# Linear attention with decay, then two MLP layers, one core: the second batch's heads of a pair exchanged

## The chip, the cores and the metric

One core of a Trainium2 chip. The metric is the device time of one execution in microseconds: median of three runs of the kernel before 559.44 us (559.34 to 560.02).

## The reference

Causal linear attention with a decay per head (2 batches, 8 heads, 768 positions, 64 channels), then two MLPs with 1536 tokens, width 512 and inner width 2048. In the reference the attention goes in blocks of 64 positions:

```python
intra = np.einsum('bhic,bhjc->bhij', qb, kb) * Dmask[None]
intra = np.einsum('bhij,bhjd->bhid', intra, vb)
inter = np.einsum('bhid,bhde->bhie', qb * lam_pow[None], kv_state)
out[:, :, sl] = intra + inter
kb_dec = kb * rev_pow[None]
kv_state = lam_block[None, :, None, None] * kv_state + np.einsum('bhsd,bhse->bhde', kb_dec, vb)
...
x = attn_out.transpose(0, 2, 1, 3).reshape(B * S, H * D)
h = x @ w_in
g = np.where(h > 0.0, h, alpha * (np.exp(np.minimum(h, 0.0)) - 1.0))
x = g @ w_out
```

`Dmask` is the head's decay `lam` to the power of the distance, zero ahead of the diagonal; the second MLP has a leaky rectifier with a slope per column in place of the exponential.

## The kernel before

**Attention.** Each batch is cut into six blocks of 128 positions; the two blocks of the same position, one of each batch, are a unit (`units`, m = 0 to 5). The host lays out keys and queries with the channels on the partitions: a pair of heads fills 128 partitions, 64 each, and `kqT` has for every block four pairs of keys and of queries (512 KB); `vk` has values and keys with the positions on the partitions (512 KB). For a unit TensorE makes:
- `scores` (L616, products L625): keys times queries, 64 channels deep, so two heads work in the two row halves of the array, each into its own bank of PSUM; VectorE multiplies with the decay masks `dm` into `sm` (L631).
- `state` (L656, L667): scaled keys `kd` times values, 64 by 64 for each head, added up in bank `SUMS`; two heads in the two column halves.
- `new_states` (L673): ScalarE or VectorE copies the sums into `st`, ScalarE multiplies the sums in PSUM by the block's decay (`decay`, L688).
- `outputs` (L691, L700): `sm` times values, two heads in the two column halves, one group for each batch, into banks `OUTS`.
- `earlier` (L707, L720): the state times the queries scaled by the decay (`qs`, L651 on GpSimd), added onto the same banks. Here `st` holds for each pair a 128 by 128 matrix with the two heads' 64 by 64 blocks on its diagonal and zeros beside them (cleared once, L762), so one product over the whole array serves both heads. Then ScalarE casts the bank to the high part of x (L419) and VectorE subtracts it for the low part (L737).

All of these are float32 products, each seen in the trace as two records. The MLP products (L872, L904, L969) use rounded high and low parts of x and weights.

**Start.** `begin` (L748) loads `lam`, spreads it with small products (L771, L773) behind six warm-up products (L609), makes the masks on VectorE (L785), gets their last row by a product (L795) and from it the query scales `qp` (L791).

**Order.** Every piece is an `Op` with a cost per engine. The planner (`Plan`) computes by when each is needed and simulates the engines; TensorE takes from the ready pieces the one needed first, and a change between kinds of array division (`mode`: full, rows, cols) costs it `CHANGE` more but is not avoided. Loads stand on the SP queue in turn: for each unit two of `kqT`, two of `vk`; only the second block's first load is on ScalarE's queue. Behind the loads of unit 3 come the first two weight loads of 1 MB (`raw`), then units 4 and 5. The first MLP's products for the chunks of units 0 to 3 are mixed into the attention; those of the third chunk (units 4 and 5, `x0`) follow it. The MLPs then run to the end.

## Time and profile before

| | |
|---|---|
| median of 3 runs | 559.44 us (559.34 to 560.02) |
| profiled execution: its time, its span | 559.58 us, 557.8 us |
| TensorE busy | 550.8 us (99%) |
| VectorE, ScalarE, GpSimd busy | 385.7, 297.8, 319.9 us |
| granted clock of TensorE | 1.00 throughout |
| chain that ended last | PE 89%, DMA 5%, VectorE 3%, ACT 2% |

An engine's busy time is the time in which at least one of its instructions runs; for TensorE ends are modelled, so the distance from start to start of two groups is what a group costs. Float32 products have two records each: 16 products are x32. The chain shows which engine the end waited for, going back step by step.

### The profile page before, as it was taken

The page shows a single profiled execution, that of the slowest core. Times are in us where ns is not written, and L with a number is a line of the kernel's source. Part 1 is how long each engine was busy: PE and PEld are TensorE (multiplying, and loading weights), DVE is VectorE, ACT ScalarE, POOL GpSimd, SP SyncE. Part 2 cuts the span into 40 slices and gives each one's busy share as a digit, 9 for nine tenths or more (in the row PEclk, how much of TensorE's full clock was granted, in tenths as well). Part 3 has the DMA queues.
Part 4 walks back from the last instruction along what each step waited for, and adds up shares of the span by engine and source line. Part 5 has one row for each costly group of instructions (what it writes and reads, how often), then busy time and mean ns, then how long its engine had stood idle before and what let it go on. Part 6 is the DMA issues. An engine that isn't in the chain of part 4 may idle for free.

```text
span 557.8 us, 7420 instructions
## 1 busy us (share of the span) xinstructions
PE 550.8 (99%) x2872; PEld 456.9 (82%) x2872; DVE 385.7 (69%) x499; ACT 297.8 (53%) x488; POOL 319.9 (57%) x222
## 2 busy tenths in 40 slices
PE   8999999999999999999999999999999999999997
PEld 6888888888888888888888887888888888888886
DVE  5688999487576867577856794649676757774554
ACT  4686776666465746556646537644454435434220
POOL 4544532676657574929368588577666583927020
PEclk9999999999999999999999999999999999999999
DMA  8992222220404132221310120032222222000114
GB/s 330 404 363 76 76 75 76 76 77 0 152 0 152 49 103 75 76 76 55 128 45 13 63 76 1 23 130 76 75 77 75 76 75 76 0 1 0 39 38 150
DMA packets 18309, 49.24 MB, mean 88 GB/s; under 512 B 1250, under 2 KB 1506, under 8 KB 18274
## 3 DMA queue, kind: packets, MB, share of 16 engines
q1 hardware_dynamic: 18128, 48.25, 24.4%
q8 instruction: 22, 0.36, 0.3%
q10 hardware_dynamic: 146, 0.52, 0.3%
q14 instruction: 13, 0.11, 0.1%
HBM read 45.62 MB, written 3.15 MB: 87 GB/s over the span
## 4 chain that ended last, share of the span: by engine, by line
PE 89%; DMA 5%; DVE 3%; ACT 2%; issue 1%; ACTq 0%; SPq 0%
PE ps L969 46%; PE ps L904 23%; PE ps L872 18%; DMA blk<-in_kqT 3%; DMA raw<-in_w1o 2%; PE ps L720 1%; PE ps L700 1%; DVE qT2l L427 1%; PE ps L625 1%; DVE g L427 1%; DVE wt L461 0%; DVE acc L981 0%; PE ps L667 0%; DVE rt L834 0%; ACT rt L817 0%
## 5 line engine op out<-in xcount | busy, mean ns | idle before, releaser
L981 DVE TENSOR_TENSOR acc<-ps,acc 128x512 f32<-128x512 f32 (+1 forms) x169 | 115.8, 687 | 93.7 <-PE ps L969 92.6
L427 POOL TENSOR_TENSOR g<-rt,g 128x512 fp32r<-128x512 f32 x86 | 123.0, 1436 | 73.6 <-ACT g L419 65.2
L969 PE MATMUL ps<-wdh,g 128*128 128x512 f32 (+1 forms) x388 | 118.5, 387 | 0.0
L969 PE MATMUL ps<-g,wdh 128*128 128x512 f32 x384 | 118.2, 389 | 0.0
L817 ACT ACTIVATE rt<-ps 128x512 f32<-128x512 f32 x96 | 57.2, 597 | 96.5 <-DVE ps L918 54.7
L969 PEld LDWEIGHTS ps<-wdh,g 128*128 128x128 f32 x388 | 72.7, 188 | 14.9
L969 PEld LDWEIGHTS ps<-g,wdh 128*128 128x128 f32 x384 | 72.1, 188 | 15.0
L419 ACT CAST g<-rt 128x512 fp32r<-128x512 f32 x96 | 59.4, 619 | 40.9 <-DVE rt L834 28.3
L969 PE MATMUL ps<-wdl,g 128*128 128x512 f32 (+1 forms) x194 | 75.0, 387 | 0.0
L969 PE MATMUL ps<-g,wdl 128*128 128x512 f32 x192 | 74.7, 389 | 0.0
L427 POOL TENSOR_TENSOR wsl<-wt,wsh 128x1024 fp32r<-128x1024 f32 x13 | 32.3, 2486 | 46.3 <-ACT wsh L419 28.5
L834 DVE SCALAR_TENSOR_TENSOR rt<-rt,beta,ps 128x512 f32<-128x512 f32 x48 | 35.6, 742 | 24.7 <-ACT rt L817 24.7
L427 POOL TENSOR_TENSOR wdl<-wt,wdh 128x1024 fp32r<-128x1024 f32 x14 | 38.4, 2746 | 20.7 <-ACT wdh L419 20.5
L461 DVE SCALAR_TENSOR_TENSOR wt<-raw,wt 128x1024 uint32<-128x1024 uint32 x32 | 45.5, 1426 | 0.0
L918 DVE TENSOR_TENSOR ps<-ps,ut 128x512 f32<-128x512 f32 x42 | 29.3, 698 | 22.8 <-PE ps L904 18.6
L427 POOL TENSOR_TENSOR wt<-wt 128x256 f32<-128x256 f32 x52 | 40.1, 784 | 8.4 <-DVE wdl L427 5.6
L458 DVE SCALAR_TENSOR_TENSOR wt<-raw,wt 128x1024 uint32<-128x1024 uint32 x32 | 42.8, 1338 | 0.2
L969 PEld LDWEIGHTS ps<-wdl,g 128*128 128x128 f32 x194 | 36.4, 188 | 7.3
L969 PEld LDWEIGHTS ps<-g,wdl 128*128 128x128 f32 x192 | 36.0, 188 | 7.5
L419 ACT COPY ut<-ps 128x512 f32<-128x512 f32 x42 | 24.6, 587 | 31.3 <-PE ps L904 31.0
L453 ACT ACTIVATE wt<-raw 128x1024 f32<-128x1024 f32 x32 | 36.6, 1143 | 8.9 <-POOL wt L427 4.1
L872 PE MATMUL ps<-x0l,wah 128*128 128x512 f32 x128 | 38.6, 389 | 0.0
(128 smaller groups left out, 929.2 us busy)
## 6 DMA issues: line engine op xcount, KB each, us to landing
raw<-in_w1i SPq DMA_DIRECT2D x8, 1024.0 KB, 5.7
raw<-in_w1o SPq DMA_DIRECT2D x8, 1024.0 KB, 4.9
raw<-in_w2i SPq DMA_DIRECT2D x8, 1024.0 KB, 5.4
raw<-in_w2o SPq DMA_DIRECT2D x8, 1024.0 KB, 4.8
blk<-in_kqT SPq DMA_DIRECT2D x11, 512.0 KB, 11.4
blk<-in_vk SPq DMA_DIRECT2D x10, 512.0 KB, 11.6
out<-acc SPq DMA_DIRECT2D x11, 256.0 KB, 2.0
blk<-in_kqT ACTq DMA_DIRECT2D x1, 512.0 KB, 4.8
```

The lines of the kernel that those rows point to most:

```text
L419: nc.scalar.copy(dst(), src())
L427: lambda e: on(e).tensor_tensor(out=dst(), in0=a(), in1=b(), op=alu),
L453: op({"ACT": 1.14}, lambda e: nc.scalar.mul(t, upper.bitcast(F32), 2.0 ** -112), [b_r], [b_t])
L458: op({"DVE": vec(1024)}, lambda e: nc.vector.scalar_tensor_tensor(out=tu, in0=lower, scalar=29, in1=tu, op0=ALU.logical_shift_right, op1=A ...
L461: op({"DVE": vec(1024)}, lambda e: nc.vector.scalar_tensor_tensor(out=tu, in0=upper, scalar=0x80000000, in1=tu, op0=ALU.bitwise_and, op1=A ...
L817: op({"ACT": act(512, True)}, lambda e: nc.scalar.activation(rt(i), h(), AF.Relu, scale=-1.0), [b_h], [b_r])
L834: op({"DVE": vec(512) + 0.06}, lambda e: nc.vector.scalar_tensor_tensor(out=rt(i), in0=rt(i), scalar=beta[:, f:f + 1], in1=h(), op0=ALU.mu ...
L872: nc.tensor.matmul(out=banks[k], lhsT=wa(s, w)[:, cc, q * 128:(q + 1) * 128], rhs=(both[t][x] if t else x0(x))[:, cc, :], start=i == 0, st ...
L904: nc.tensor.matmul(out=banks[k], lhsT=left(s, a, w)[:, cc, :], rhs=quad(b, x)[:, cc, :], start=bool(opens and i == 0), stop=bool(closes an ...
L918: op({"DVE": vec(512)}, lambda e: nc.vector.tensor_tensor(out=banks[to], in0=banks[k], in1=ut(u), op=ALU.add), [b_ps[k], b_ut[u]], [b_ps[to]])
L969: nc.tensor.matmul(out=p_, lhsT=lhs, rhs=rhs, start=i == 0, stop=i == 5)
L981: op({"DVE": vec(w)}, lambda _, a=a, p_=p_: nc.vector.tensor_tensor(out=a(), in0=p_, in1=a(), op=ALU.add), [b_ps[k], *b_a], b_a)
```

## The change

The heads of a pair are exchanged for the second batch: head `hs` lies on partitions `half(hs ^ b)`. A head's state is kept as its 64 by 64 block alone; the product with the queries uses a quarter of the array for each head and batch, so that the two batches and two heads of a pair fill four quarters (`earlier`; five groups of 16 products for ten of 4). Scores are cut into halves of the keys in the same way (12 groups of 16 products for 12 of 8). The states are copied in one instruction; the decay takes eight instructions of 64 columns for four of 128; masks' last row and query scales are made once for each batch. The second batch's keys and queries come in two loads of 64 partitions, all on the SP queue, with `alpha` behind unit 3; half of the warm-up products follow the spreading of `lam`. The planner lets TensorE prefer a piece of the present mode if it is needed at most `STAY` (2 us) later than another.

```diff
-    FREE = True
+    STAY = 2.0
...
-                if e == "PE" and self.FREE:
-                    while ready[e]:
-                        op = heapq.heappop(ready[e])[2]
-                        if op not in begun:
...
                 if e == "PE":
-                    if at < len(pe) and not left[pe[at]]:
-                        shift = now - first[pe[at]]
-                        begin(e, pe[at])
-                        at += 1
+                    queue = [item for item in ready[e] if item[2] not in begun]
+                    if queue:
+                        op = min(queue, key=lambda item: (
+                            item[0] + self.STAY * (item[2].mode != mode), item[1]))[2]
+                        shift = now - first[op]
+                        ready[e] = [item for item in queue if item[2] is not op]
+                        begin(e, op)
...
-    lams_sb = sb("lams_sb", [H + NP])
-    lam_sb, lamp = lams_sb[:, 0:H], lams_sb[:, H:H + NP]
+    lams_sb = sb("lams_sb", [H + B * NP])
+    lam_sb, lamp = lams_sb[:, 0:H], lams_sb[:, H:].rearrange("p (b a) -> p b a", b=B)
...
-    st = low[:, 2:4].rearrange("p b (a i) -> p b a i", a=NP)
+    st = low[:, 2].rearrange("p (b a d) -> p b a d", b=B, a=NP)
     top = sb("qpsm", [3, 512], F32, "ut")
-    qp = top[:, 0].rearrange("p (a i) -> p a i", a=NP)
-    lamc = qp[:, :, C - 1:C]
+    qps = [x.rearrange("p (a i) -> p a i", a=NP) for x in (top[:, 0], low[:, 3])]
...
-
-        def load_kq(self, queue="SP"):
-            load(self.kq, kqT[self.n], 0.5, [self.b_kq], queue, True)
-
-        def load_vk(self, queue="SP"):
+            self.rows = [half(hs ^ b) for hs in range(2)]
+
+        def load_kq(self):
+            if self.n < PB:
+                load(self.kq, kqT[self.n], 0.5, [self.b_kq], turn_=True)
+                return
+            parts = []
+            for hs in range(2):
+                x = Buf()
+                x.wrote, x.read = list(self.b_kq.wrote), list(self.b_kq.read)
+                load(self.kq[self.rows[hs]], kqT[self.n, half(hs)], 0.25, [x], turn_=True)
+                parts += x.wrote
+            self.b_kq.wrote, self.b_kq.read = parts, []
+
+        def load_vk(self):
             n = 1 if self.n % PB == PB - 1 else 2
-            load(self.vk[:, 0:n], vk[self.n, :, 0:n], 0.25 * n, [self.b_v], queue, True)
...
-                    for hs in range(2):
+                    for hs, s in ((0, 0), (1, 1), (0, 1), (1, 0)):
                         nc.tensor.matmul(
-                            out=banks[ks[hs]][:, pr * C:(pr + 1) * C],
-                            lhsT=x.kq[half(hs), 0, pr, :], rhs=x.kq[half(hs), 1, pr, :],
-                            start=True, stop=True)
-            pe(0.89, run, [x.b_kq], [b_ps[k] for k in ks], 32, "rows")
+                            out=banks[ks[hs]][half(s), pr * C:(pr + 1) * C],
+                            lhsT=x.kq[x.rows[hs], 0, pr, half(s)],
+                            rhs=x.kq[x.rows[hs], 1, pr, :], start=True, stop=True)
+            pe(0.86, run, [x.b_kq], [b_ps[k] for k in ks], 64, "quarters")
...
-                        in0=x.kq[:, 1], in1=qp, op=ALU.mult)
-                op(SCALE, queries, [x.b_kq, b_qp], [b_qs[m % 2][b]], True)
+                        in0=x.kq[:, 1], in1=qps[b], op=ALU.mult)
+                op(SCALE, queries, [x.b_kq, b_qp[b]], [b_qs[m % 2][b]], True)
...
-                            out=view[half(hs), b, pr, :],
+                            out=view[x.rows[hs], b, pr, :],
...
-        parts = []
-        for hs in range(2):
-            x = Buf()
-            x.wrote, x.read = list(b_st.wrote), list(b_st.read)
-            copy(lambda hs=hs: st[half(hs), :, :, half(hs)], lambda hs=hs: view[half(hs)],
-                 [b_ps[SUMS]], [x], 512, True)
-            parts += x.wrote
-        b_st.wrote, b_st.read = parts, []
+        copy(lambda: st, lambda: view, [b_ps[SUMS]], [b_st], 512, True)
         if m < UNITS - 2:
             def decay(e):
-                for pr in range(NP):
-                    nc.scalar.mul(view[:, :, pr, :], view[:, :, pr, :], lamc[:, pr, :])
-            op({"ACT": 1.05}, decay, [b_ps[SUMS], b_qp], [b_ps[SUMS]])
+                for b in range(B):
+                    for pr in range(NP):
+                        nc.scalar.mul(view[:, b, pr, :], view[:, b, pr, :], qps[b][:, pr, C - 1:C])
+            op({"ACT": 1.6}, decay, [b_ps[SUMS], *b_qp], [b_ps[SUMS]])
...
-        for b in range(B):
-            k = ks[b]
-            if m:
-                def run(b=b, k=k):
-                    for pr in range(NP):
-                        nc.tensor.matmul(
-                            out=banks[k][:, pr * C:(pr + 1) * C], lhsT=st[:, b, pr, :],
-                            rhs=qss[m % 2][:, b, pr * C:(pr + 1) * C],
-                            start=False, stop=True, skip_group_check=True)
-                pe(0.88, run, [b_st, b_qs[m % 2][b]], [b_ps[k]], 16)
+        if m:
+            def run():
+                for pr in range(NP):
+                    for hs in range(2):
+                        for b, x in enumerate(units[m]):
+                            nc.tensor.matmul(
+                                out=banks[ks[b]][half(hs), pr * C:(pr + 1) * C],
+                                lhsT=st[x.rows[hs], b, pr, :],
+                                rhs=qss[m % 2][x.rows[hs], b, pr * C:(pr + 1) * C],
+                                start=False, stop=True, skip_group_check=True)
+            pe(0.86, run, [b_st, *b_qs[m % 2]], [b_ps[k] for k in ks], 64, "quarters")
+        for b, k in enumerate(ks):
...
-        op({"POOL": 1.1}, lambda e: nc.gpsimd.memset(st, 0.0), [], [b_st])
...
-            for hs in range(2):
-                nc.tensor.matmul(
-                    out=p_[half(hs), H:H + NP], lhsT=row[:, 0:64],
-                    rhs=lams.rearrange("p (a s) -> p s a", s=2)[:, hs], start=True, stop=True,
-                    skip_group_check=True)
-        pe(0.4, spread, [b_row, b_one], [b_ps[k]])
-        run_up(3)
-        op({"DVE": 0.17}, lambda e: nc.vector.tensor_copy(lams_sb, p_[:, 0:H + NP]),
+            for b in range(B):
+                for hs in range(2):
+                    nc.tensor.matmul(
+                        out=p_[half(hs ^ b), H + b * NP:H + (b + 1) * NP], lhsT=row[:, 0:64],
+                        rhs=lams.rearrange("p (a s) -> p s a", s=2)[:, hs], start=True, stop=True,
+                        skip_group_check=True)
+        plan.behind(pe(0.4, spread, [b_row, b_one], [b_ps[k]]), run_up(3))
+        op({"DVE": 0.17}, lambda e: nc.vector.tensor_copy(lams_sb, p_[:, 0:H + B * NP]),
...
-        def powers(e):
-            for pr in range(NP):
-                nc.scalar.mul(qp[:, pr], p2[:, pr * C:(pr + 1) * C], lamp[:, pr:pr + 1])
-
-        def last_row():
-            for hs in range(2):
-                nc.tensor.matmul(
-                    out=p2[half(hs)], lhsT=last_key, rhs=dm[:, hs].rearrange("p a i -> p (a i)"),
-                    start=True, stop=True, skip_group_check=True)
         for hs in range(2):
             op({"DVE": 1.3}, lambda e, hs=hs: masks(e, hs), [b_lam, b_anti], [b_dm[hs]], True)
-        k2 = turn("ps", 8)
-        p2 = banks[k2]
-        pe(1.0, last_row, [*b_dm, b_last], [b_ps[k2]], 8, "cols")
-        op({"ACT": 1.05}, powers, [b_ps[k2], b_lam], [b_qp])
-        load(alpha_sb, alpha, 0.01, [b_alpha])
+        for b in range(B):
+            k = turn("ps", 8)
+            p2 = banks[k]
+
+            def last_row(b=b, p2=p2):
+                for hs in range(2):
+                    nc.tensor.matmul(
+                        out=p2[half(hs ^ b)], lhsT=last_key,
+                        rhs=dm[:, hs].rearrange("p a i -> p (a i)"), start=True, stop=True,
+                        skip_group_check=True)
+
+            def powers(e, b=b, p2=p2):
+                for pr in range(NP):
+                    nc.scalar.mul(qps[b][:, pr], p2[:, pr * C:(pr + 1) * C], lamp[:, b, pr:pr + 1])
+            pe(0.9, last_row, [*b_dm, b_last], [b_ps[k]], 8, "cols")
+            op({"ACT": 1.05}, powers, [b_ps[k], b_lam], [b_qp[b]])
...
         def fetch(m):
-            for i, x in enumerate(units[m]):
-                x.load_kq("ACT" if m == 0 and i else "SP")
+            for x in units[m]:
+                x.load_kq()
             for x in units[m]:
                 x.load_vk()
         begin()
         for m in range(4):
             fetch(m)
+        load(alpha_sb, alpha, 0.01, [b_alpha], turn_=True)
```

TensorE's queue, the piece with the state products of units 1 and 2 (scores L625, outputs L700, states L667, state products L720); before:

```order
L720 MATMUL ps<-qs,dmst 128x128 x4
L667 MATMUL ps<-blk,kd 64x64 x16
L625 MATMUL ps<-blk 128x128 x8
L720 MATMUL ps<-qs,dmst 128x128 x4
L625 MATMUL ps<-blk 128x128 x8
L700 MATMUL ps<-sm,blk 64x128 x8
L625 MATMUL ps<-blk 128x128 x8
L700 MATMUL ps<-sm,blk 64x128 x8
L720 MATMUL ps<-qs,dmst 128x128 x4
L667 MATMUL ps<-blk,kd 64x64 x16
L720 MATMUL ps<-qs,dmst 128x128 x4
L700 MATMUL ps<-qpsm,blk 64x128 x8
```

and now (scores L630, outputs L699, states L672, state products L719):

```order
L630 MATMUL ps<-blk 64x128 x32
L699 MATMUL ps<-sm,blk 64x128 x8
L672 MATMUL ps<-blk,kd 64x64 x16
L719 MATMUL ps<-qs,dmst 64x128 x16
L630 MATMUL ps<-blk 64x128 x32
L699 MATMUL ps<-sm,blk 64x128 x16
L719 MATMUL ps<-qs,dmst 64x128 x16
L672 MATMUL ps<-blk,kd 64x64 x16
L699 MATMUL ps<-qpsm,blk 64x128 x8
L699 MATMUL ps<-sm,blk 64x128 x8
L719 MATMUL ps<-qs,dmst 64x128 x16
L672 MATMUL ps<-blk,kd 64x64 x16
```

The state products of both batches stand in one group, and groups of scores and of outputs stand together.

ScalarE's queue around the casts of units 1 and 2 (key scaling L641, casts L419, decay L688); before:

```order
L641 ACTIVATE kd<-blk,dmst 128x64 x8
L419 CAST qbh<-ps 128x4x128
L419 COPY dmst<-ps 64x8x64
L419 CAST qbh<-ps 128x4x128
L641 ACTIVATE kd<-blk,dmst 128x64 x8
L688 ACTIVATE ps<-ps,qpsm 128x2x64 x4
L453 ACTIVATE wt<-raw 128x1024
L419 CAST qbh<-ps 128x4x128
```

and now (key scaling L646, casts L411, decay L687):

```order
L646 ACTIVATE kd<-blk,dmst 128x64 x8
L411 CAST qbh<-ps 128x4x128 x2
L687 ACTIVATE ps<-ps,qpsm 128x64 x4
L687 ACTIVATE ps<-ps,dmst 128x64 x4
L646 ACTIVATE kd<-blk,dmst 128x64 x8
L411 CAST qbh<-ps 128x4x128 x2
L445 ACTIVATE wt<-raw 128x1024
L687 ACTIVATE ps<-ps,qpsm 128x64 x4
```

Both casts of a unit stand together, and those of unit 2 stand behind eight key scalings (of unit 3).

SP's queue from its start; before:

```order
L407 DMA alpha_sb<-in_alpha 128x16
L407 DMA blk<-in_kqT 128x1024
L407 DMA blk<-in_vk 128x1024 x2
L407 DMA blk<-in_kqT 128x1024 x2
L407 DMA blk<-in_vk 128x1024 x2
L407 DMA blk<-in_kqT 128x1024 x2
```

and now:

```order
L399 DMA blk<-in_kqT 128x1024
L399 DMA blk<-in_kqT 64x1024 x2
L399 DMA blk<-in_vk 128x1024 x2
L399 DMA blk<-in_kqT 128x1024
L399 DMA blk<-in_kqT 64x1024 x2
L399 DMA blk<-in_vk 128x1024 x2
```

Keys of both batches come first, the second's in two loads of 64 partitions, and `alpha` has gone behind unit 3.

## Rows read from the trace of the kernel before

**Rows 1.** Windows of core 0: length, busy us by engine (records), granted clock, DMA share, GB/s.

```profile
0.00:5.80 5.80, 3.66 (x18) 3.32 (x18) 1.11 (x5) 1.49 (x2) 1.87 (x9) 1.00 0.63 213
5.80:58.18 52.38, 51.16 (x664) 43.47 (x665) 40.94 (x62) 35.18 (x90) 27.19 (x20) 1.00 0.77 300
58.18:100.00 41.82, 41.82 (x185) 34.46 (x184) 39.52 (x48) 30.43 (x51) 14.54 (x10) 1.00 0.19 64
```

**Rows 2.** Timeline, TensorE: start us, us, line, shape, records, wait; the start.

```profile
1.18 2.93 PE L609 MATMUL ps<-warm 128*128 128x128 f32 x12 [1.18 <-DVE warm L750]
4.04 0.59 PE L771 MATMUL ps<-row 1*128 1x8 f32 x2
...
5.80 2.06 PE L625 MATMUL ps<-blk 64*128 64x128 f32 x32 [0.96 <-DMA blk<-in_kqT]
7.79 1.14 PE L795 MATMUL ps<-dmst,last_key 128*64 128x512 f32 x4
```

**Rows 3.** Timeline, TensorE, the end of the attention stage.

```profile
50.70 1.15 PE L667 MATMUL ps<-blk,kd 128*64 128x64 f32 x32
51.69 1.05 PE L700 MATMUL ps<-qpsm,blk 128*64 128x128 f32 x16
52.56 1.04 PE L700 MATMUL ps<-sm,blk 128*64 128x128 f32 x16
...
55.34 1.17 PE L872 MATMUL ps<-qbh,wah 128*128 128x512 f32 x4
...
58.18 1.07 PE L872 MATMUL ps<-x0h,wah 128*128 128x512 f32 x4
```

**Rows 4.** Waits to 60 us, TensorE's: who for whom, us in total, times, longest.

```profile
PE ps L625 <- DMA blk<-in_kqT: 1.4, 3, 1.0
...
PE ps L667 <- ACT ps L688: 0.3, 1, 0.3
...
PE ps L700 <- DVE sm L631: 0.2, 1, 0.2
```

**Rows 5.** Windows of core 0, columns as in rows 1, two while all loads run.

```profile
20.00:25.00 5.00, 5.00 (x86) 4.57 (x88) 2.88 (x5) 3.25 (x12) 3.60 (x3) 1.00 1.03 399
25.00:30.00 5.00, 5.00 (x82) 4.35 (x79) 3.43 (x7) 4.14 (x12) 1.06 (x1) 1.00 1.04 407
```

**Rows 6.** Timeline, TensorE: state products (L720) and unit 4's first scores.

```profile
18.79 1.16 PE L720 MATMUL ps<-qs,dmst 128*128 128x128 f32 x8
19.88 1.15 PE L667 MATMUL ps<-blk,kd 128*64 128x64 f32 x32
...
32.03 1.16 PE L625 MATMUL ps<-blk 64*128 64x128 f32 x16 [0.23 <-DMA blk<-in_kqT]
...
45.97 2.05 PE L720 MATMUL ps<-qs,dmst 128*128 128x128 f32 x16
47.78 1.17 PE L872 MATMUL ps<-qbh,wah 128*128 128x512 f32 x4
```

**Rows 7.** Timeline, VectorE: the masks, and a subtraction of low parts.

```profile
5.16 2.63 DVE L785 TENSOR_TENSOR_SCAN dmst<-lams_sb,anti 128x128 f32<-128x128 f32 x8
...
25.31 0.68 DVE L737 TENSOR_TENSOR qbl<-ps,qbh 128x512 fp32r<-128x512 f32 x1
```

**Rows 8.** Timeline, GpSimd: key scaling of unit 3.

```profile
25.58 1.06 POOL L644 TENSOR_TENSOR kd<-blk,dmst 128x512 f32<-128x512 f32 x1 [0.96 <-DMA blk<-in_vk]
```

**Rows 9.** Timeline, ScalarE: powers, cast of an output, key scaling, decay.

```profile
9.42 1.11 ACT L791 ACTIVATE qpsm<-ps,lams_sb 128x128 f32<-128x128 f32 x4
...
23.78 0.58 ACT L419 CAST qbh<-ps 128x512 fp32r<-128x512 f32 x1
24.26 2.02 ACT L641 ACTIVATE kd<-blk,dmst 128x64 f32<-128x64 f32 x8
26.18 1.44 ACT L688 ACTIVATE ps<-ps,qpsm 128x128 f32<-128x128 f32 x4
```

**Rows 10.** The page, DMA issues: KB each, median us from issue to landing.

```profile
blk<-in_kqT SPq DMA_DIRECT2D x11, 512.0 KB, 11.4
```

More of the change, by code (lines that the diff above doesn't have):

```diff
@@ L120, in simulate @@
     def simulate(self, first, back=False, log=None):
-        pe = self.pe[::-1] if back else self.pe
         before = (lambda op: op.after) if back else (lambda op: op.before)
@@ L131, in simulate @@
         events, begun, n = [], {}, 0
-        at, done, now, dma, shift = 0, 0, 0.0, 0.0, -first[pe[0]]
+        done, now, dma, shift = 0, 0.0, 0.0, -first[self.pe[-1 if back else 0]]
         stock, seen, mode = self.AHEAD, 0.0, None
@@ L137, in offer @@
             for e in op.costs:
-                if e != "PE" or self.FREE:
-                    heapq.heappush(ready[e], (first[op], n, op))
-                    n += 1
+                heapq.heappush(ready[e], (first[op], n, op))
+                n += 1
         def wake(t, what=None):
@@ L184, in simulate @@
                     continue
-                if e == "PE" and self.FREE:
-                    while ready[e]:
-                        op = heapq.heappop(ready[e])[2]
-                        if op not in begun:
-                            shift = now - first[op]
-                            begin(e, op)
-                            break
-                    continue
-                if e == "PE":
-                    if at < len(pe) and not left[pe[at]]:
-                        shift = now - first[pe[at]]
-                        begin(e, pe[at])
-                        at += 1
+                if e == "PE":
+                    queue = [item for item in ready[e] if item[2] not in begun]
[5 more added lines that the diff above has]
+                        begin(e, op)
                     continue
@@ L573, in attention_two_layers @@
     b_dm = [Buf(), Buf()]
-    b_qp, b_lam, b_anti, b_warm, b_row = (Buf() for _ in range(5))
+    b_qp = [Buf() for _ in range(B)]
+    b_lam, b_anti, b_warm, b_row = (Buf() for _ in range(4))
     SUMS = 6
@@ L584, in attention_two_layers, with half @@
     PART = [1, 1, 2, 2, 0, 0]
+    def half(x):
+        return slice(x * 64, (x + 1) * 64)
     class Block:
@@ L593, in __init__ @@
             self.n = PB * b + m
-        def load_kq(self, queue="SP"):
-            load(self.kq, kqT[self.n], 0.5, [self.b_kq], queue, True)
-        def load_vk(self, queue="SP"):
+            self.rows = [half(hs ^ b) for hs in range(2)]
[11 more added lines that the diff above has]
+        def load_vk(self):
             n = 1 if self.n % PB == PB - 1 else 2
-            load(self.vk[:, 0:n], vk[self.n, :, 0:n], 0.25 * n, [self.b_v], queue, True)
+            load(self.vk[:, 0:n], vk[self.n, :, 0:n], 0.25 * n, [self.b_v], turn_=True)
     units = [[Block(m, b) for b in range(B)] for m in range(UNITS)]
@@ L610, in run @@
                     out=banks[k][:, 0:128], lhsT=warm, rhs=warm, start=True, stop=True)
-        pe(0.22 * n, run, [b_warm, *reads], [b_ps[k]])
-    def half(x):
-        return slice(x * 64, (x + 1) * 64)
+        return pe(0.22 * n, run, [b_warm, *reads], [b_ps[k]])
     def scores(m):
@@ L1076, in build @@
             for e in range(4):
-                b_acc[0, e, q].read += old(*b_dm, b_st)
+                b_acc[0, e, q].read += old(*b_dm, b_st, b_qp[1])
         for b in b_ut:
-            b.read += old(b_qp, *b_sm[2])
+            b.read += old(b_qp[0], *b_sm[2])
         b_wa[1][1].read += old(*b_sm[3])
```

## The prediction

> **What bounds the kernel now.** I read the windows first [rows 1]. From 58.18 us on TensorE works without a gap (41.82 us busy of 41.82 to 100 us), so whatever is taken from TensorE's work ahead of 58.18 us moves the end by the same amount, unless something new makes it wait. Ahead of that lies the attention stage, from the first scores at 5.80 us [rows 2] to the first product of the third token chunk at 58.18 us [rows 3]: 52.38 us, in which TensorE is busy for 51.16. The reader is to see that this stage is also bound by TensorE, but only just. The waits there [rows 4] are small (1.4 us for `kqT`, 0.96 of it ahead of the first scores, 0.3 for ACT's decay, 0.2 for the masked scores), yet the DMA engines are full (share 1.03, 399 GB/s from 20 to 25 us [rows 5]), and the scores of unit 4 begin the moment their keys land, at 32.03 us [rows 6]. So less work on TensorE is a gain as far as the loads let it through.
>
> **Prices.** State products (L720): two groups of four take 47.78 − 45.97 = 1.81 us, 0.905 a group [rows 6]. Alone, between other kinds of product, a group takes 19.88 − 18.79 = 1.09 us [rows 6]; the 0.185 us more is the price of a change of the array's division. The other ends of that price: a group at L667 costs 50.70 to 51.69 = 0.99 where the next has the same division, and 1.09 − 0.99 is about 0.1. I take 0.185, the price at the very groups that change, and keep 0.1. Outputs (L700): 52.56 − 51.69 = 0.87; states (L667): 0.99 for 32 records [rows 3]. Scores (L625): two groups in 7.79 − 5.80 = 1.99 with one change, so 0.90 each [rows 2].
>
> A group in quarters is in no row. Sixteen products of 128 columns, four at a time, stream for as long as eight that go two at a time: 0.87 to 0.90. It issues 32 records, and L667's 32 records need 0.99, so that is the other end for full concurrency. I take 0.93, nearer to the streams since these have 128 columns and not 64. If only two quarters run at a time, it is 1.8, twice a group of scores (a rival below).
>
> **The sum, part by part.**
> 1. State products: ten groups at 0.905 become five at 0.93: 9.05 − 4.65 = −4.4 us.
> 2. Scores: twelve groups from 0.90 to 0.93: +0.4 (ends −0.4 and +1.1).
> 3. The second product of the masks' last row (L795): 1.14 us for both heads with its end [rows 2], 0.95 without it: +0.95.
> 4. Changes of division between the first scores and the third W1 tile of the stage: I count 33 in the order before and 23 in the new one (11 and 7 in the pieces shown with the change). Ten at 0.185: −1.85 (end −1.0).
> 5. Start. The first 5.80 us move 213 GB/s [rows 1], 1.24 MB, of which the first two loads of keys are 1.05. Now these stand first in one queue, with no `alpha` ahead of them and no values beside them: 0.19 MB at 399 GB/s is 0.5 us. Half of the 2.93 us of warm-up goes behind the lam product (4.04 us [rows 2]), so the masks (5.16 to 7.79 us [rows 7]) start up to 1.4 us earlier too. I take −0.5; ends 0 and −1.0.
> 6. Waits. Before, the work in the stage is 10.8 scores + 0.95 + 10.44 outputs (12 × 0.87) + 4.95 states + 9.05 + the three W1 tiles (36 products; one takes 58.18 − 55.34 = 2.84 us [rows 3], 0.1 of it the change ahead: 8.2 in all) + 33 × 0.185 = 50.5 us; the stage lasts 52.38, so 1.9 are waits, listed or too short to be. After, the same list gives 11.16 + 1.9 + 10.44 + 4.95 + 4.65 + 8.2 + 4.26 = 45.6. New waits come from the loads: 2.1 MB a unit at 399 GB/s is 5.3 us, while a unit now needs some 6.2 us of TensorE (two scores 1.86, two outputs 1.74, state 0.99, state products 0.93, 3.5 changes 0.65), so only the first units and unit 4 meet them. And one comes from ACT's queue: its casts of unit 2 stand behind eight key scalings of unit 3, as today, but are wanted sooner. The scalings wait for values landing at 25.58 us (POOL's L644 of the same unit ends its wait there [rows 8]). 25.58 + 2.02 (L641) + two casts of 0.58 [rows 9] + VectorE's L737, 0.68 [rows 7], is 29.4 us, less the 0.5 of the start: 28.9. Only then is the output bank free for unit 3. TensorE gets there at 5.3 + 8 × 0.93 + 1.9 + 6 × 0.87 + 3 × 0.99 + 2 × 0.93 + 11 × 0.185 = 26.7 us, with a microsecond of waits for the keys of units 1 and 2 at 27.7: a wait of 1.2 more. I put the new waits at 3.0 in place of 1.9: +1.1 (ends 0 and +2.5).
>
> Sum: −4.4 + 0.4 + 0.95 − 1.85 − 0.5 + 1.1 = **−4.3 us**.
>
> What costs nothing: ACT's decay becomes eight instructions of half the width; four take 1.44 us [rows 9], so eight lie between 1.44 and 2.9, one more microsecond on the way from one state to the next, of which one copy of 0.58 is given back. TensorE waits for the decay 0.3 us in all today [rows 4], so this hides; without that cover it would be 0.4 to 0.9 us a unit. The second powers (L791, 1.11 us [rows 9]) stand ahead of ACT's first cast, where the keys of unit 1 are waited for anyway. SP issues seven loads more (six by the halving, one that was ACT's), and its loads of keys are issued 11.4 us ahead of their landing [rows 10]. GpSimd's clearing of the states stood ahead of an idle stretch.
>
> The profiled execution took 559.58 us (span 557.8), 0.14 above the median of 559.44. 559.58 − 4.3 is 555.3, or **555.2** against the median. Its own range, from the ends above: 553.4 to 557.3.
>
> **Rivals.**
> *The half loads run at half rate.* Each 512 KB of the second batch's keys is now two loads onto 64 rows. A 128-row load takes 1.31 us at 399 GB/s. If a half, which reaches half of the rows, is no faster than that, each unit gets 1.31 us longer, 6.6 us until both halves for unit 4 are there: 32.03 + 1.3 (the second batch) − 0.5 + 6.6 = 39.4 us. After that there remain three groups of scores, four of outputs, a state, two groups of state products, eight changes and the three W1 tiles: 2.8 + 3.5 + 1.0 + 1.9 + 1.5 + 8.2 = 18.9. That ends at 58.3, where TensorE stands today at 58.18: the whole gain is gone, **560** with a wait or two. For it: nothing in the trace, which has no 64-row load. Against it: the rate is the same 399 to 407 GB/s whether keys, values or weights are moved, in loads of 512 KB or 1 MB [rows 5], so bytes alone have set it so far. Since no row decides it and any rate between is possible, I give it 0.27, over 557.5 to 561. The Trainium skill has a rule that is this rival ("SBUF — State Buffer", Door 1: The DMA port swizzle): 64 rows reach half of the ports, and two transfers onto the two halves serialize. By that rule the time is the 560; no run here shows it yet.
>
> *Quarters run only two at a time* (the rival that ends slower). Place: every group of scores, 12 × (1.8 − 0.9) = +10.8; state products 5 × 1.8 against 9.05, no gain; +0.95 − 1.85 − 0.5, and about 1 us of waits less: +8.4, **568**. It decides from about 1.2 us a group on. For it: no row has rows and columns divided at once. Against it: L625 divides rows, L700 columns, and both run two at a time. In part it may hold for the state products alone, whose two row halves write one bank in turn: then only the 4.4 us go, 559. The Trainium skill has a rule of that kind ("TensorEngine Tiling (Array Packing)", Gotcha 1: PSUM Pressure: different row tiles cannot access the same bank at the same time); by it the time is that 559, and nothing in the trace speaks to it. 0.06 for each.
>
> *VectorE becomes the bound.* From 58.18 to 100 us it is busy 39.52 of 41.82 us [rows 1], so TensorE, 4 us ahead, may run into it: in full that takes back 2 to 4 us, **557.5 to 559.5**. Against it: VectorE is idle for a fifth of the stage before (40.94 of 52.38 [rows 1]) and no wait for it is seen today. 0.10.
>
> *The change doesn't do what it says:* that the new order brings none of the merging is excluded by its rows; 0.01.
>
> **How the numbers follow.** Forecast 0.50. A measurement of this kernel tells 0.2% (1.1 us) from no change, so faster is below 558.3. Forecast 0.50, a third of the half-rate case (0.09), two thirds of VectorE's (0.07): 0.66. Same: 0.10 of the half-rate case, the rest of VectorE's and the one-bank case: 0.19. Slower: 0.08 of the half-rate case and the quarters, 0.15. The range 553.4 to 560.6 leaves out the quarters, the end of the half-rate case and a few hundredths below.
>
> **What would show it.** Right: first scores near 5.3 us; a group of 32 state-product records and of 32 score records at 0.93, 1.1 with a change; outputs of unit 3 waiting for L738 about a microsecond; the stage over near 54 us; no gap behind it. Wrong: waits of TensorE for `kqT` of a microsecond or more in each unit (half rate), quarter groups of 1.3 us or more, or gaps behind 60 us that VectorE ends.

## The result and the profile after

The changed kernel takes **568.36 us** (median of 5 runs, 566.43 to 569.45) against 559.65 for the kernel before beside it: a ratio of 1.0150 (95% interval 1.0132 to 1.0169), 8.7 us slower. The forecast was 555.2 us with a range up to 560.6: the time went the other way and left the range. The profiled execution took 569.45 us.

The page of the changed kernel: span, busy times, the rate in 40 slices of the span, the chain that ended last, and the loads of keys and queries (KB each, median us to landing):

```profile
span 566.5 us, 8025 instructions
...
PE 551.4 (97%) x3152; PEld 455.2 (80%) x3152; DVE 393.7 (69%) x501; ACT 301.1 (53%) x509; POOL 320.8 (57%) x220
...
GB/s 264 292 319 242 48 67 75 75 75 74 2 148 93 56 75 74 75 75 76 76 146 1 75 67 8 2 148 5 144 75 74 75 74 75 1 1 0 38 38 148
...
PE 82%; DMA 9%; DVE 5%; issue 1%; ACT 1%; SPq 1%; ACTq 0%; DVEq 0%
...
blk<-in_kqT SPq DMA_DIRECT2D x6, 512.0 KB, 10.1
blk<-in_kqT SPq DMA_DIRECT2D x12, 256.0 KB, 12.5
```

TensorE is busy about as long as before (550.8 then), the span is 8.7 us longer: the time went into waiting. The chain's share of DMA rose from 5 to 9%. A load of half the bytes lands later after its issue (12.5 us) than one of 512 KB before (11.4 [rows 10]).

TensorE's waits in it to 82 us (who waited for whom: us in total, times, longest; those under 0.6 left out):

```profile
PE ps L630 <- DMA blk<-in_kqT: 3.7, 5, 1.7
PE ps L672 <- issue: 1.9, 1, 1.9
PE ps L699 <- DVE qbl L738: 1.5, 1, 1.5
...
PE ps L630 <- DVE qpsm L636: 0.9, 1, 0.9
PE ps L874 <- DVE rt L832: 0.8, 2, 0.5
PE ps L874 <- DVE x0l L738: 0.7, 1, 0.7
PE ps L971 <- DVE rt L832: 0.6, 1, 0.6
```

Where [rows 4] had 1.4 us for `kqT` there are 3.7, and a new kind: "issue", a gap for which the profile shows no releaser.

Its timeline of TensorE (start us, us, line, operands, records, wait ahead):

```profile
5.38 3.76 PE L630 MATMUL ps<-blk 64*64 64x128 f32 x64
9.07 2.04 PE L797 MATMUL ps<-dmst,last_key 128*64 128x512 f32 x8
...
15.46 1.15 PE L672 MATMUL ps<-blk,kd 128*64 128x64 f32 x31
18.49 0.27 PE L672 MATMUL ps<-blk,kd 128*64 128x64 f32 x1 [1.88 <-issue]
...
19.66 3.79 PE L630 MATMUL ps<-blk 64*64 64x128 f32 x64
23.39 1.09 PE L699 MATMUL ps<-sm,blk 128*64 128x128 f32 x16
...
33.50 1.10 PE L719 MATMUL ps<-qs,dmst 64*64 64x128 f32 x32
34.53 1.15 PE L672 MATMUL ps<-blk,kd 128*64 128x64 f32 x32
...
49.08 1.10 PE L630 MATMUL ps<-blk 64*64 64x128 f32 x32 [1.66 <-DMA blk<-in_kqT]
...
64.90 1.07 PE L874 MATMUL ps<-x0h,wah 128*128 128x512 f32 x4
66.64 1.20 PE L874 MATMUL ps<-x0l,wah 128*128 128x512 f32 x4 [0.67 <-DVE x0l L738]
```

A state-product group of 32 records takes 34.53 − 33.50 = 1.03 us with its change of division, 0.85 without (0.185): four quarters do run at once, since two at a time would be some 1.8. The third chunk's first product starts at 64.90 us, 6.7 later than in [rows 3]. The gap of 1.88 us stands in the middle of one group, 31 records ahead of it and one behind, and the profile shows nothing that this one record waited for. And the scores at 19.66 us take 3.73 for what takes 1.9 elsewhere: the granted clock there is the next view's.

Windows of the changed kernel (columns as in [rows 1]): just behind that gap; a 128-row load of keys; the two 64-row loads behind it; two weight loads. Which load runs follows from the bytes moved in the order of issue.

```profile
19.00:22.00 3.00, 3.00 (x52) 2.69 (x51) 0.30 (x1) 2.69 (x9) 1.45 (x2) 0.59 1.01 318
...
22.20:23.40 1.20, 1.20 (x32) 1.03 (x24) 0.79 (x2) 0.67 (x3) 0.89 (x1) 0.68 1.06 416
23.60:26.00 2.40, 2.26 (x56) 2.05 (x56) 1.18 (x2) 1.15 (x5) 1.06 (x1) 1.00 1.03 191
30.00:35.00 5.00, 4.80 (x110) 4.07 (x112) 1.39 (x3) 2.86 (x11) 2.29 (x2) 1.00 1.05 398
```

The DMA engines are full in all four (1.01 to 1.06). The 64-row loads move 191 GB/s, the 128-row load and the weights 416 and 398: each engine is as busy and moves half. (The first window, with 318, has the end of two half loads and values in it.) By the DMA view about as many packets pass in the 2.40 us of the 64-row loads (139) as in the 1.20 us of the 128-row one (133). After 1.88 us without work the granted clock fell (0.59 from 19 to 22 us: mostly 1.2 GHz, the lower of the two levels).

### The profile page after: what moved, and what is told of

Read it like the earlier page. It is cut to its first block, busy times and chain, and to the rows that moved or that the text cites. A ratio compares the mean times of both kernels' runs of the same rounds, so it can differ in the third digit from the quotient of the medians.

```text
span 566.5 us, 8025 instructions
## 1 busy us (share of the span) xinstructions
PE 551.4 (97%) x3152; PEld 455.2 (80%) x3152; DVE 393.7 (69%) x501; ACT 301.1 (53%) x509; POOL 320.8 (57%) x220
## 4 chain that ended last, share of the span: by engine, by line
PE 82%; DMA 9%; DVE 5%; issue 1%; ACT 1%; SPq 1%; ACTq 0%; DVEq 0%
PE ps L971 45%; PE ps L906 23%; PE ps L874 14%; DMA blk<-in_kqT 5%; DMA raw<-in_w1i 2%; DMA blk<-in_vk 2%; DVE g L419 1%; DVE wt L453 1%; SPq L399 1%; DVE qT2l L419 1%; DVE x0l L738 0%; DVE acc L983 0%; DVE rt L836 0%; DVE rt L832 0%; ACT rt L819 0%
## 5 line engine op out<-in xcount | busy, mean ns | idle before, releaser
L419 POOL TENSOR_TENSOR g<-rt,g 128x512 fp32r<-128x512 f32 x83 | 119.1, 1443 | 70.9 <-ACT g L411 68.9
L411 ACT CAST g<-rt 128x512 fp32r<-128x512 f32 x96 | 59.3, 619 | 44.0 <-DVE rt L836 28.3
L419 POOL TENSOR_TENSOR wsl<-wt,wsh 128x1024 fp32r<-128x1024 f32 x13 | 32.3, 2488 | 44.0 <-ACT wsh L411 26.2
L453 DVE SCALAR_TENSOR_TENSOR wt<-raw,wt 128x1024 uint32<-128x1024 uint32 x32 | 48.0, 1501 | 0.1
L419 POOL TENSOR_TENSOR wt<-wt 128x256 f32<-128x256 f32 x51 | 38.2, 762 | 15.5 <-DVE wdl L419 7.4
L419 POOL TENSOR_TENSOR wdl<-wt,wdh 128x1024 fp32r<-128x1024 f32 x14 | 37.7, 2696 | 14.9 <-ACT wdh L411 14.7
L411 ACT COPY ut<-ps 128x512 f32<-128x512 f32 x41 | 24.1, 588 | 37.5 <-PE ps L906 35.0
L450 DVE SCALAR_TENSOR_TENSOR wt<-raw,wt 128x1024 uint32<-128x1024 uint32 x32 | 43.2, 1352 | 0.2
L419 POOL TENSOR_TENSOR wal<-wt,wah 128x1024 fp32r<-128x1024 f32 x13 | 33.1, 2544 | 15.6 <-ACT wah L411 15.6
## 6 DMA issues: line engine op xcount, KB each, us to landing
blk<-in_kqT SPq DMA_DIRECT2D x12, 256.0 KB, 12.5
```

Source lines behind the costliest of these rows:

```text
L411: nc.scalar.copy(dst(), src())
L419: lambda e: on(e).tensor_tensor(out=dst(), in0=a(), in1=b(), op=alu),
L450: op({"DVE": vec(1024)}, lambda e: nc.vector.scalar_tensor_tensor(out=tu, in0=lower, scalar=29, in1=tu, op0=ALU.logical_shift_right, op1=A ...
L453: op({"DVE": vec(1024)}, lambda e: nc.vector.scalar_tensor_tensor(out=tu, in0=upper, scalar=0x80000000, in1=tu, op0=ALU.bitwise_and, op1=A ...
```

## The experiments

All ratios are to the kernel before on the same chip (medians 559.63 to 559.77). "Kept order" means that every engine does the same pieces in the same order as in the kernel compared with; in the other runs the planner lays the order anew.

| run | what it is | median us | ratio (95%) |
|---|---|---|---|
| bsplit | before + 64-row loads | 570.68 | 1.0203 (1.0184–1.0222) |
| cols | change, two loads of 128 rows; kept order | 560.40 | 1.0016 (1.0007–1.0024) |
| whole | change, single loads | 562.46 | 1.0049 (1.0030–1.0068) |
| twoq | change, second halves on ScalarE's queue | 576.39 | 1.0285 (1.0251–1.0319) |
| warm | change, old warm-up; kept order | 569.05 | 1.0166 (1.0150–1.0183) |
| wwarm | whole, old warm-up; kept order | 561.91 | 1.0041 (1.0027–1.0055) |
| wfree | whole, `STAY` 0 | 560.68 | 1.0011 (1.0003–1.0020) |
| srow | whole, scores in rows as before | 556.82 | 0.9946 (0.9934–0.9958) |
| arow | change, scores in rows | 568.52 | 1.0160 (1.0147–1.0173) |
| qscore | before + scores in quarters | 564.14 | 1.0067 (1.0054–1.0081) |
| wrow | whole, scores in rows; kept order | 559.81 | 1.0001 (0.9992–1.0010) |
| srowq | srow, scores in quarters; kept order | 560.08 | 1.0010 (1.0000–1.0019) |
| srowq45 | the same for units 4 and 5 alone | 557.34 | 0.9953 (0.9941–0.9965) |
| bq | before, scores in quarters; kept order | 559.41 | 0.9994 (0.9985–1.0002) |
| srowfree | srow, `STAY` 0 | 559.22 | 0.9988 (0.9978–0.9998) |
| srowwarm | srow, old warm-up | **556.32** | 0.9939 (0.9928–0.9951) |

### Loads onto 64 rows

*whole* and *cols*: the host's layout exchanges the halves (`kq[PB:] = np.concatenate([kq[PB:, 64:], kq[PB:, :64]], axis=1)`), so that a block comes in one load, or in two that are cut by columns:

```diff
-                load(self.kq[self.rows[hs]], kqT[self.n, half(hs)], 0.25, [x], turn_=True)
+                load(self.kq[:, hs], kqT[self.n, :, hs], 0.25, [x], turn_=True)
```

> The changed kernel with the second batch's halves exchanged in the input's layout, so that each of its six kqT blocks comes as one 128-row load again; nothing else is changed, though the planner lays the order anew. Theory A (64-row loads run at half rate): the twelve half loads took 3.07 MB at about 220 GB/s where 128-row loads run at about 405, that is 6.4 us of loading; chunk 3's products go from 64.9 back to about 58 us and the time from 568.4 to 554 to 559. Theory B (the clock and the new start of the warm-up are to blame): 566 to 568. Theory C (the merged order of modes makes VectorE the bound, whatever the loads): 563 to 567, with VectorE busy over 9.8 of 10 us in 60 to 70 as in the changed kernel.

> As the run with single loads, but each of the six kqT blocks of the second batch still comes as two loads of 256 KB on SP, cut by columns (keys, then queries) over all 128 rows; the order on TensorE is the changed kernel's, row for row. Theory A (64 rows are what is slow): rate 380 to 415 GB/s while they run, time 555 to 560. Rival D (two transfers of 256 KB instead of one, that is their number and size, are slow, or SP's eight transfers under way): the rate stays at 200 to 250 GB/s and the time at 566 to 569. Theories B and C: 564 to 568.

*bsplit* puts the loads' loop of the change into the kernel before, with rows in their own halves:

```diff
-            load(self.kq, kqT[self.n], 0.5, [self.b_kq], queue, True)
+                load(self.kq[rows], kqT[self.n, rows], 0.25, [x], queue, True)
```

> The kernel before with one edit: the second batch's six kqT blocks come as two 64-row loads each, no heads exchanged, products and modes as before. Theory A: 3.07 MB at about 220 instead of 400 GB/s costs 6.3 us of loading, and the time goes from 559.6 to 563 to 568. Theories B and C: within 0.5 us of 559.6, as nothing that they name is touched.

Timeline of *cols*, a pair of score groups and the third chunk's first product:

```profile
17.49 1.98 PE L630 MATMUL ps<-blk 64*64 64x128 f32 x64
19.40 1.09 PE L699 MATMUL ps<-sm,blk 128*64 128x128 f32 x16
...
58.46 1.07 PE L874 MATMUL ps<-x0h,wah 128*128 128x512 f32 x4
```

Windows of *cols*, in the second the two 256 KB loads of unit 3, in the third weights:

```profile
18.70:20.00 1.30, 1.30 (x40) 1.13 (x33) 1.30 (x3) 1.20 (x6) 0.81 (x1) 1.00 1.00 399
20.00:21.40 1.40, 1.37 (x39) 1.23 (x35) 1.13 (x2) 1.40 (x7) 0.51 (x1) 1.00 1.06 391
24.10:29.30 5.20, 3.60 (x95) 3.18 (x88) 4.28 (x7) 4.93 (x18) 3.54 (x3) 1.00 1.04 394
```

Windows of *bsplit*, 128 rows and then 64:

```profile
21.90:23.10 1.20, 1.20 (x12) 1.05 (x12) 0.40 (x1) 0.72 (x3) 0.81 (x1) 1.00 1.02 406
23.40:25.20 1.80, 1.80 (x45) 1.61 (x39) 0.30 (x1) 1.47 (x6) 1.06 (x1) 1.00 1.07 221
```

As many loads of as many bytes run at 391 GB/s if they reach 128 rows. With every other instruction where it was, that gives back 568.36 − 560.40 = 8.0 us (6.8 against the changed kernel's two runs at a granted clock of 0.999 and 1.00, 567.17; no run of *cols* was lower); in the kernel before the 64-row loads alone cost 11.0, more than the 3 to 8 expected. So it is the rows, not the number or size of the loads, and neither of the two rivals in these expectations, which name the start and the merged order, explains the 8.0 us. The rule of the Trainium skill that the forecast named as a rival ("SBUF — State Buffer", Door 1: The DMA port swizzle: 64 rows reach half of the ports) agrees with the 191 to 221 GB/s here.

But *whole*, expected at 554 to 559, and *cols*, just outside 555 to 560, gain nothing over the kernel before. A second loss is left.

*twoq*: `("SP", "ACT")[hs]` as the queue of the two halves.

> The changed kernel (568.4 us) with the second half of each split load issued from ScalarE's queue, so that the two halves of a block can be under way together; products and planner as in the change. If a 64-row load is slow because it uses one half of the rows' way into the memory, two opposite halves together move 350 to 410 GB/s and the time is 559 to 564. If each 64-row load costs every engine double whatever runs beside it: 200 to 250 GB/s as before, 566 to 571.

The DMA view of *twoq* from 7 to 11 us, with halves on ScalarE's queue (q10) beside SP's loads (q1):

```profile
DMA packets 274, 0.98 MB, mean 245 GB/s; under 512 B 35, under 2 KB 35, under 8 KB 274
...
q1 hardware_dynamic: 142, 0.52, 54.5%
q10 hardware_dynamic: 132, 0.46, 50.0%
```

Two queues share the engines, the sum stays low. That the two halves of one block ran together is not seen in it, and ScalarE's loads also stood behind its own work, so the time, slower than either expectation (single runs 571.69 to 581.45 us), tells nothing about the halves.

### The start

*warm* (and *wwarm*, *srowwarm*) put the six warm-up products together again:

```diff
-        plan.behind(pe(0.4, spread, [b_row, b_one], [b_ps[k]]), run_up(3))
+        pe(0.4, spread, [b_row, b_one], [b_ps[k]]); run_up(3)
```

> The changed kernel with the start's old order alone: all six warm-up products ahead of the lambdas' spread, as before; every other instruction in the changed kernel's order, half loads included. Theory B (the spread between the warm-up's products keeps TensorE at half clock over the first scores, which took 3.69 us for 64 products): the first scores take 2.2 to 2.4 us, and the time falls by 1 to 2 us to 566.4 to 567.4. Theory A: the first scores may be faster, but the loads set the stage's end, so 567.8 to 568.8.

> Single loads, and the six warm-up products together ahead of the lambdas' spread as before; every other instruction stands as in the run with single loads (562.5 us). Theory B (the new start keeps the clock at its lower level through the first scores, which took 2.8 to 3.7 us for 64 records where 2.0 is due): the first scores take 2.0 to 2.2 us and the time falls by 1 to 2 us to 560.5 to 561.5. Theory E: no change beyond 0.5 us, 562 to 563; the first scores may still be slow.

> The run with single loads, scores as before and the states' products in quarters (556.8 us), with the six warm-up products together ahead of the lambdas' spread. Theory B (the order of the warm-up holds the clock down in the first scores, 3.79 us for 32 records where before took 2.06): 555 to 556. If the order of the warm-up is not what decides: 556.5 to 557.5.

−0.5 us in the two runs with single loads and +0.7 in *warm*, each near the range that was expected of no effect. The first scores stay slow: 64 records in 3.5 us in *wwarm* (1.98 in *bq*), 32 in 3.7 in *srowwarm* (2.0 before [rows 2]). So the new order of the warm-up isn't it. In *bsplit*, whose start is that of before, the first scores are slow too (18 records in 2.50 us, then a wait of 1.97 for `kqT`); in *bq* they are not. In *whole* they take 2.7 us, in the changed kernel 3.69, and the profile's granted clock is 1.00 over them (window 5.38 to 9.07 us), so no row shows a lower clock as the cause. What decides it stays open; up to 1.7 us hang on it.

### The scores in quarters

*srow* and *arow* emit the scores as before:

```diff
-                    for hs, s in ((0, 0), (1, 1), (0, 1), (1, 0)):
+                    for hs in range(2):
                         nc.tensor.matmul(
-                            out=banks[ks[hs]][half(s), pr * C:(pr + 1) * C],
-                            lhsT=x.kq[x.rows[hs], 0, pr, half(s)],
+                            out=banks[ks[hs]][:, pr * C:(pr + 1) * C],
+                            lhsT=x.kq[x.rows[hs], 0, pr, :],
...
-            pe(0.86, run, [x.b_kq], [b_ps[k] for k in ks], 64, "quarters")
+            pe(0.89, run, [x.b_kq], [b_ps[k] for k in ks], 32, "rows")
```

> Single 128-row loads, the states' products in quarters as in the change, and the scores as before (8 products of 128x128 in two row halves for a batch, not 16 in quarters); the order is planned anew. Theory E (TensorE runs out of instructions: while the loads fill the DMA engines a packet of 16 KB of instructions comes every 6.3 us at best, and its reading products stop in the middle of a group with the releaser given as issue, 3.0 us in all in each of the two runs with 128-row loads): this takes 192 of the 280 added matmul records out, so the gaps given as issue fall under 0.7 us and the time to 556 to 559. Theory B (the start's clock): 560 to 562, since the start is that of the single-load run. Theory D (the merging of modes is what costs): 560 to 563.

> The changed kernel with its split loads (568.4 us) and the scores alone as before. Theory E (too many instructions for what the fetch brings while loads run, 5.6 us between the two runs with single loads): if it adds to the loads' cost, 562 to 565; if TensorE waits for the late loads anyway, so that the missing instructions cost nothing there, 566 to 569.

*srow* is 3.0 us faster than the kernel before and 5.6 faster than *whole*: with the scores in rows the change pays, with the scores in quarters it doesn't. In the changed kernel itself the scores' quarters cost nothing (*arow*): there TensorE waits for the loads anyway (6.8 us for `kqT` in *arow*, 3.7 in the changed kernel). Timeline of *srow*, the third chunk's first product, 3.0 us ahead of [rows 3]:

```profile
55.15 1.07 PE L874 MATMUL ps<-x0h,wah 128*128 128x512 f32 x4
```

*qscore* makes the opposite edit in the kernel before (quarters, and 64 and "quarters" told to the planner); *wfree* and *srowfree* set `STAY` to 0.

> The kernel before with one edit: the scores in quarters (64 records instead of 32 for a unit of two batches), in the array's mode of their own; states, loads, heads, start and planner as before. Theory E: 288 instructions instead of 224 for a unit in some 7.7 us of products stand close to what a packet of 256 in 6.3 us feeds; gaps given as issue of 0 to 1.5 us, and with 12 groups at 0.03 us more each the time is 559.8 to 561.5. If instructions cost nothing: 559.4 to 560.2.

> Single loads, and the planner's preference for staying in a mode at 0 instead of 2 (the order by due time alone, as the planner before had it); the products are the change's. Theory D (merging makes groups wait for each other: L699 behind VectorE's qbl 3.5 us in the run with single loads): those waits fall under 1 us, more changes of mode at 0.19 each come back, 557 to 560. Theory E: the gaps given as issue stay at 2 to 3.5 us whatever the order, and the time at 560 to 563.

> The run with single loads, scores as before and the states' products in quarters (556.8 us), with the planner's preference for a mode at 0 instead of 2. If merging saves what the forecast took (about ten changes of mode at 0.185 us): 558 to 559. If it is worth nothing or less, as with the scores in quarters, where taking it away gave 562.5 to 560.7: 555 to 557.

*qscore* fell outside its range, and its longest wait is no issue gap (TensorE's waits, two of its lines):

```profile
PE ps L969 <- DVE acc L421: 2.6, 1, 2.6
...
PE ps L667 <- issue: 0.5, 1, 0.5
```

So the planner's new order might be the cause, not the instructions. By the medians merging is worth 2.4 us with scores in rows (*srowfree* − *srow*), but −1.8 with scores in quarters (*wfree* − *whole*), where the gaps given as issue are 2.8 us in *wfree* as well; a part of both figures is the granted clock, as shown below. To separate them, the last four runs keep the order and change only the products: *wrow* emits rows while the planner is told of quarters, *srowq*, *srowq45* and *bq* the reverse.

> The run with single loads (562.5 us), its order kept row for row on every engine (the planner is still told of quarters), while the scores' products are emitted as before, in row halves of 128x128. Theory E (too many instructions for the fetch): the gaps given as issue, 3.0 us, go, with the falls of the clock that follow on TensorE's idle time, and the time is 557 to 560. Rival O (the order laid for quarters is bad): the waits for qbl of 3.5 us and for acc of 1.4 us stay, and the time is 561 to 563.

> The run with single loads and scores as before (556.8 us), its order kept row for row, while the scores' products are emitted in quarters. Theory E: gaps given as issue come up again, 2 to 4 us in all by 40 us, and the time is 559 to 562. Rival O: within 0.7 us of 556.8.

> As srowq, but only the scores of units 4 and 5 are emitted in quarters, 64 more matmul records from about 32 us on, where the block loads are nearly done; units 0 to 3 as before. Theory E, which needs the loads beside the products: gaps given as issue of 0 to 0.5 us and a time of 556.3 to 557.5. If quarters cost by themselves, wherever they stand: a third of what srowq adds, 557.5 to 558.5.

> The kernel before with the scores emitted in quarters and its order kept row for row (the run that also told the planner of it had 564.1). Theory E: 288 instructions for a unit against some 250 in the same time by the fetch: gaps of 0.5 to 2 us, 560 to 562. Rival O: 559.4 to 560.2, so that the 564.1 was the planner's new order.

Quarters against rows in one order: 562.46 − 559.81 = 2.7 us, and 560.08 − 556.82 = 3.3. In units 4 and 5 alone 0.5; in the order of the kernel before nothing (559.41 against 559.76). There the expected gaps did not come and the rival's range was met: the 4.7 us of *qscore* over *bq* are the planner's new order. The other 3.0 of *whole*'s loss (559.81 − 556.82) come with the order that was laid for quarters. Timeline of *srowq*, its three gaps given as issue (this execution took 562.21 us, 2.1 above the median):

```profile
16.66 0.38 PE L630 MATMUL ps<-blk 64*64 64x128 f32 x2 [0.93 <-issue]
...
22.95 0.33 PE L672 MATMUL ps<-blk,kd 128*64 128x64 f32 x3 [1.08 <-issue]
...
29.34 0.54 PE L699 MATMUL ps<-sm,blk 128*64 128x128 f32 x5 [1.60 <-issue]
```

They end 6.3 and 6.4 us apart, in scores, states and outputs alike, each inside a group. The DMA view counts one packet of instructions in each of the windows 20 to 21.5 and 26.5 to 28 us:

```profile
q8 instruction: 1, 0.02, 4.6%
```

The same two gaps, with a packet in the same two windows, are in *cols*:

```profile
22.73 0.33 PE L672 MATMUL ps<-blk,kd 128*64 128x64 f32 x3 [1.36 <-issue]
...
29.12 0.54 PE L699 MATMUL ps<-sm,blk 128*64 128x128 f32 x5 [1.60 <-issue]
```

Between them TensorE does 3 + 32 + 64 + 27 = 126 products' records and as many weight loads, 252 instructions, with one packet. *srow*, *wrow* and *srowq45* have no such gap. So TensorE runs out of instructions. The traces tie each stop to a packet: the nine gaps given as issue in *srowq*, *cols*, *whole* and the changed kernel all end 1.3 to 1.6 us after a packet is through; and the page counts 22 of these packets before and 24 in the changed kernel, which has 560 instructions of TensorE more. A unit asks for 2 × 64 in scores, 2 × 32 in outputs, 64 in states and 64 in state products, 320 in the 6.2 us that part 6 of the forecast gives it; with scores in rows it is 256, and in *srow* packets come 6.2 and 6.4 us apart without a gap. In the kernel before, quarters make it 288 in a longer unit.

Why a packet comes no sooner is not shown. It was argued that the full DMA engines hold it up; that was not varied by itself. For it speaks that no gap given as issue stands behind the loads and that 64 records in units 4 and 5 cost 0.5 us; against it, that from 33 us on the next packet comes after 5.0 us in *cols* and 4.2 in *srowq*, with the engines still full (0.96 to 1.07 of their time to 37 us).

The forecast could have read this price in the code: the planner of both kernels counts each piece's instructions (`steps`, 64 for a group in quarters, 32 in rows), supplied at `FETCH` = 45 a us with at most `AHEAD` = 384 in stock. In these stretches 252 in 6.3 us are 40 a us.

*whole*'s order has a further price, in TensorE's waits (its profiled execution took 564.67 us, 2.2 above its median):

```profile
PE ps L699 <- DVE qbl L738: 3.5, 2, 3.0
PE ps L971 <- DVE acc L413: 1.4, 1, 1.4
```

and a window behind the 3.0 us wait (granted clock 0.50):

```profile
36.00:38.00 2.00, 2.00 (x32) 2.00 (x30) 2.00 (x3) 2.00 (x6) 1.42 (x2) 0.50 0.89 341
```

In *wrow* these two waits are still 2.8 and 1.4 us.

Behind such waits the clock falls as well, and each run's granted clock tells where. *srow*, *cols* and *wfree* stayed at 0.998 or more in every run. *whole* did in two of six (560.99 and 561.09 us; the others, at 0.994 to 0.997, took 561.82 to 564.67), *wrow* in one of 11 (558.26; the others 558.67 to 560.67), *srowfree* in three of 12 (557.48 to 557.84; the others 558.83 to 560.48, and in the profiled one of these the clock is 0.50 behind a wait of 2.1 us for ScalarE's decay). At the full clock merging is worth 0.9 us with scores in rows (557.70 − 556.82) and −0.4 with scores in quarters (560.68 − 561.04).

From the kernel before to the changed one, by the medians: −2.9 (*srow*) + 3.0 (order laid for quarters) + 2.7 (instructions) − 2.1 (*cols* − *whole*: two loads a block and the order laid for them) + 8.0 (64 rows) = +8.7. By the runs at full clock alone, few as they are: −2.9 + 1.4 + 2.8 − 0.6 + 6.8 = +7.5. So half of the order's 3.0 and most of the −2.1 come from runs in which the clock fell; whether the wait ahead of the fall was longer in them too, one profile of each kernel doesn't show.

## Why the prediction was wrong, point by point

1. **Loads, the step that failed.** Part 6 took 2.1 MB a unit at 399 GB/s, half loads included. They ran at 191 GB/s (221 in *bsplit*), and with 128 rows in their place the time falls by 8.0 us. The argument for the 399, "the same 399 to 407 GB/s whether keys, values or weights are moved", came from 128-row loads alone: rows of one shape can't tell what another shape costs, and the rule that did speak of 64 rows got 0.27. The rival's own working was close on the loads (6.6 us later; measured 64.90 against 58.46 us for the third chunk in *cols*, 6.4). It still gave 560, because it set the whole gain of 4.3 against it, which was not there, and nothing for what lateness does behind the stage: TensorE waits 1.2 us for VectorE after 64.9 us (0.67 shown above, 0.55 at 77.45); VectorE is busy for all of the 6.90 us ahead of that, which speaks for its having to catch up.
2. **Scores (part 2), the second.** Forecast +0.4 for 0.93 a group. The products are cheaper: in *cols* two groups take 1.91 us, one change in it, 0.86 each. But I priced 32 records by their time alone, not as instructions to be supplied: 2.7 to 3.3 us, and 3.0 for the order, with the runs in which the clock falls. No row of before has an issue gap, so the bound could not be read there; but the planner's `steps` and `FETCH` stood in the code, and a step that doubles a group's instructions should have widened the term.
3. **State products (part 1), right in the price of a group**: 1.03 with a change. No run varies them alone; *srow*'s −2.9, with 1.7 lost at the start, fits the forecast's sum without the scores, −4.7, as a whole.
4. **Last row (part 3), right**: 9.07 to 11.11 us for two pairs, 0.9 more than one.
5. **Changes of division (part 4), too large**: 0.9 at the full clock for a forecast 1.85 (2.4 by the medians, with the runs of *srowfree* in which the clock falls), and −0.4 with scores in quarters.
6. **Start (part 5), wrong**: scores began at 5.38 us as forecast (5.3) but took 3.69 for 1.98: +1.3 at 9.07 instead of −0.5.
7. **Rivals.** Quarters two at a time: its 568 is the measured time, by chance; the groups take 1.03, also for state products whose two row halves write one bank, so the rule of the Trainium skill that the forecast weighed ("TensorEngine Tiling (Array Packing)", Gotcha 1: PSUM Pressure) doesn't bind here. VectorE as the bound: 1.2 us of it, as a result of the lateness. The wait of part 6 that comes from ScalarE's queue is there: the outputs wait 1.45 us for L738 (forecast 1.2).

## What to carry to other kernels

Cut a load along its columns, not to 64 of the 128 rows; where halves must be exchanged, exchange them in the layout in memory. *srowwarm* does that, keeps the scores in rows and the states' products in quarters, and beats both kernels (556.32 us). Where products get smaller, count TensorE's instructions per microsecond, and look for gaps in the middle of a group. Compare the granted clock of each run before a difference of medians is put down to an order. To tell a step's price from the planner's new order, tell the planner the old cost and change only what is emitted.

## What the runs showed of the hardware that I had not expected

- A load onto 64 rows moves 191 to 221 GB/s with all DMA engines at 1.03 to 1.07 of their time; 128 rows 391 to 416, in loads of 256 KB to 1 MB.
- From 16 to 30 us, while all loads run, TensorE gets some 250 instructions in 6.3 us (*srowq*, *cols*); where it is asked for more it stops for 0.6 to 1.9 us at a time, under the name "issue", until 1.3 to 1.6 us after a packet of instructions is through.
- After a stop of 1.9 us (change), 2.0 (*wrow*), 2.1 (*srowfree*) or 3.0 us (*whole*) the granted clock was 0.50 in a window of 2 us behind it, the lower of the two levels, and in the changed kernel 64 score records took 3.73 us instead of 1.9.
